# Denominators of a linear attention: summed on VectorE after a trip through DRAM, in place of a matmul

## The chip, the cores and the metric

The kernel runs on one core of one Trainium2 chip. Time is device microseconds of one execution; the verdicts compare medians of several executions of the two kernels on the same chip. Engines are named as in the profile: PE (TensorE), PEld (its weight loads), DVE (VectorE), ACT (ScalarE), POOL (GpSimd) and SP (SyncE). DVE, ACT, POOL and SP each work their instructions off in order. SP and ACT both issue DMAs; q1 is the queue of those from SP, q10 the queue of those from ACT.

## The reference

`x` is 2048 tokens of width 640. Two branches are computed from it and mixed by a gate for each token. Branch A is a linear attention with 32 heads of width 20; branch B is a token-shift MLP with two layer norms (hidden width 1728).

```
q, k, v = split(x @ wqkv);  phi(t) = where(t > 0, t+1, exp(t)) + 1e-6
kv  = sum over s of phi(k)[s,d] * v[s,e]           (a 20x20 matrix for each head)
z   = sum over s of phi(k)[s]                      (20 numbers for each head)
den = sum over d of phi(q)[s,d] * z[d] + 1e-6      (one number for each token and head)
a   = concat(phi(q) @ kv / den) @ wo
h   = gelu(layernorm(x) @ w1); four channel groups shifted by +1, -1, +2, -2 tokens
x1  = x + h_shifted @ w2;  b = x1 + gelu(layernorm(x1) @ w3) @ w4
out = g*a + (1-g)*b,  g = sigmoid(x . gate_w)
```

The change touches how `den` is summed.

## The kernel before

The tokens are 16 chunks of 128, in 4 tiles of 512 (index `t`, chunk `cc` in it). The program is written in the order in which each engine runs it; nothing is rescheduled. The stages follow each other on PE: `k_mm`, `q_unit`, `g_unit` (x against phi(k)), `w1_unit` for tiles 0 and 1 with `kv_unit` and `m_unit` (the folded matrix kv*wo in six groups) between them, `w2_unit(0, cc)`, `w1_unit` for tiles 2 and 3, and then for each tile the loop of `w3_unit`, with the next tile's `w2_unit` and this tile's `att_unit` between its pieces, and `w4_turned`.

phi(q) lies with features on partitions: partition `p` of chunk `j` (`j` is 0 to 4) holds feature 5p+j, so a head takes four neighbouring partitions. `den_add(j)` adds `z`-weighted chunks into `u`, 128 partitions x 2048 tokens of float32, which lies in the first two fifths of `xT`, out of use by then. What is left is a sum over each head's four partitions.

Before the change PE makes that sum. `den_hi` (ACT, L263) and `den_lo` (DVE, L266) split `u` into two bfloat16 parts in `xT`. `den_mm` (L272) multiplies both with the 0/1 mask `hm_bf`, built on POOL at the start, four tiles at once into four column groups of the array. `den_evac` (DVE, L278) adds 1e-6 into an `x1` buffer, with 32*t + head on partitions. `den_recip` (DVE, L283) inverts it into `r_bf`, `r_spread` copies it to `r4` on 32 partitions (DVE, L287), and four DMAs (L289) put each head's row on its four partitions in `rb`. `scale_t(0)` (DVE, L293) multiplies phi(q) of tile 0 with it, and `att_unit(0, 0)` (L518) is the first to read that.

Around these steps:

- `m_unit(g)` ends in a copy on ACT (L431). `m_store` writes the six results to DRAM (L435), `m_load` fetches them back in the layout that `att_unit` needs (L441).
- `ln1_apply` for chunks 14 and 15 runs on ACT (L329). Each normalized chunk goes through a DMA transpose issued by SP (L333) into `lnxT`, the input of `w1_unit(3)` (L396). `ln2_apply` (DVE, L504) does the same for `w3_unit` (L506, L537).
- `w4_sb` is loaded after `r_spread` (L654 to L656) and first read by `w4_turned(0)` (L568), which also needs `h2x`, transposed by a DMA at L556.
- `w4_sb` and the `x1` buffers lie over `xT` and its neighbours, so they wait for the last use of those.
- Each DMA takes the next of eight semaphores in turn, and waits until the DMA eight before it has landed.

Of the kernel before, what the change touches and what calls it, by code (L numbers as in the profile page):

```python
# [8 lines left out]
ALU = mybir.AluOpType  # L9
BF16 = mybir.dt.bfloat16  # L10
F32 = mybir.dt.float32
# [5 lines left out]
def kernel(  # L17
# [13 lines left out]
    nc = tc.nc  # L31
    P = 128
    S, D = A_x.shape[1], A_x.shape[2]
    F = B_w3.shape[1]
    H, Dh = 32, 20
    NCH = S // P
    TS = 512
    NT = S // TS
    CPT = TS // P
    DC = D // P  # L40
    HD = D // 2
    FF = F // P
    FR = F - FF * P
    EPS = 1e-5
    CG = D // 4
# [3 lines left out]
    GW = GH * Dh  # L49
    NG = 6  # L50
    row0 = [g * GW for g in range(5)] + [D - P]
# [9 lines left out]
    const = ctx.enter_context(tc.tile_pool(name="const", bufs=1))  # L61
# [4 lines left out]
    ps = ctx.enter_context(tc.tile_pool(name="ps", bufs=4, space=PSUM))  # L66
    dram = ctx.enter_context(tc.tile_pool(name="dram", bufs=1, space=bass.MemoryType.DRAM))
    m_dram = dram.tile([NG, P, D], BF16)

    def pair():  # L70
        return ps.tile([P, 2, 512], F32, name="pp")
# [7 lines left out]
    w2_sb = const.tile([P, DC, D], BF16)  # L79
    w3_sb = const.tile([P, DC, F], BF16)  # L80
    wo_sb = const.tile([P, NG, D], BF16)
# [8 lines left out]
    g5 = const.tile([DC, P], BF16)  # L90
    g5z = const.tile([P, P], BF16)
    mhalf = const.tile([P, CPT], F32)
    hmask = const.tile([P, H], F32)
    z = const.tile([P, DC], F32)
    hm_bf = const.tile([P, H], BF16)
    bmask = const.tile([P, GH * 4], F32)
    bmask5 = const.tile([P, 8], F32)
    ylog = const.tile([P, NCH], F32)
# [15 lines left out]
    xT = st1.tile([P, DC, S], BF16)  # L114
# [27 lines left out]
    load_x(2, 16)  # L142
    sp.dma_start(wv_sb[:], wqkv_v[:, :, 2 * D:3 * D])
    sp.dma_start(w1_sb[:], B_w1.rearrange("(c p) f -> p c f", p=P))
    for g in range(NG):
        sp.dma_start(wo_sb[:, g, :], A_wo[row0[g]:row0[g] + P, :])
    sp.dma_start(w2_sb[:, 0:2, :], B_w2[0:2 * CG, :].rearrange("(g p) f -> p g f", g=2)[0:P])
    for g in range(2, 4):
        sp.dma_start(w2_sb[:, g, :], B_w2[CG * g:CG * g + P, :])
    sp.dma_start(w2_sb[:, 4, :], B_w2.rearrange("(g p) f -> g p f", g=4)[:, P:CG, :])  # L150
    sp.dma_start(w3_sb[:], B_w3.rearrange("(c p) f -> p c f", p=P))

# [4 lines left out]
                            base=0, pattern=[[-1, P]], channel_multiplier=1)  # L157
    for c in range(0, NCH, CPT):
        nc.gpsimd.memset(x_sb[:, c:c + CPT, D:D + 1], 1.0)
    nc.gpsimd.memset(hmask[:], 1.0)  # L160
    nc.gpsimd.affine_select(out=hmask[:], in_=hmask[:], compare_op=ALU.is_ge, fill=0.0,
                            base=0, pattern=[[-4, H]], channel_multiplier=1)
    nc.gpsimd.affine_select(out=hmask[:], in_=hmask[:], compare_op=ALU.is_ge, fill=0.0,
                            base=3, pattern=[[4, H]], channel_multiplier=-1)
    nc.gpsimd.tensor_copy(hm_bf[:], hmask[:])
    for m, n, off in ((bmask, GH, 0), (bmask5, 2, 88)):
        nc.gpsimd.memset(m[:], 1.0)
        nc.gpsimd.affine_select(out=m[:], in_=m[:], compare_op=ALU.is_ge, fill=0.0,
# [90 lines left out]
            else:  # L259
                nc.vector.scalar_tensor_tensor(u[:, sl], pqT[:, j, sl], z[:, j:j + 1], u[:, sl], op0=ALU.mult, op1=ALU.add)  # L260

    def den_hi(sl):
        nc.scalar.copy(xT[:, 4, sl], u[:, sl])  # L263

    def den_lo(sl):
        nc.vector.tensor_tensor(xT[:, 3, sl], u[:, sl], xT[:, 4, sl], op=ALU.subtract)  # L266

    def den_mm():
        pt = pair()
        for n in range(2):  # L270
            for t in range(NT):
                nc.tensor.matmul(pt[32 * t:32 * (t + 1), 0, :], lhsT=hm_bf[:], rhs=xT[:, 4 - n, t * TS:(t + 1) * TS],  # L272
                                 start=(n == 0), stop=(n == 1))
        return pt

    def den_evac(pt):
        d = x1p.tile([P, D], F32, name="x1")[:, 0:TS]
        nc.vector.tensor_scalar_add(d, pt[:, 0, :], 1e-6)  # L278
        return d

    def den_recip(d):
        with nc.allow_low_precision(reason="rounded after a float32 division, as a copy would"):
            nc.vector.reciprocal(r_bf[:], d)  # L283
# [39 lines left out]
    def ln1_apply(c, eng=nc.vector):  # L323
        t, cc = divmod(c, CPT)
        if cc == 0:
            lnxT[t] = lnx_p.tile([P, DC, TS], BF16, name="lnxT")
        lnx = work.tile([P, D], BF16, name="ln")
        if eng is nc.scalar:
            nc.scalar.activation(lnx[:], x_sb[:, c, 0:D], ACT.Identity, bias=nmr1[:, c:c + 1], scale=rstd1[:, c:c + 1])  # L329
        else:  # L330
            nc.vector.tensor_scalar(lnx[:], x_sb[:, c, 0:D], mv1[:, c, 0:1], rstd1[:, c:c + 1],
                                    op0=ALU.subtract, op1=ALU.mult)
        nc.sync.dma_start_transpose(lnxT[t][:, :, cc * P:(cc + 1) * P], lnx[:])  # L333
# [92 lines left out]
    def m_unit(g):  # L426
        pt = pair()
        for hf in range(2):
            nc.tensor.matmul(pt[:, hf, 0:HD], lhsT=kvT[:, row0[g]:row0[g] + P],  # L429
                             rhs=wo_sb[:, g, hf * HD:(hf + 1) * HD], start=True, stop=True)  # L430
        nc.scalar.copy(mst[g // 2][:, g % 2, :].rearrange("p (h e) -> p h e", h=2), pt[:, :, 0:HD])  # L431

    def m_store():
        for i in range(NG // 2):
            nc.sync.dma_start(m_dram[2 * i:2 * i + 2].rearrange("g p e -> p g e"), mst[i])  # L435
# [7 lines left out]

    for fcs in w1_split:
        w1_unit(0, fcs)
    for sl in halves:
        den_hi(sl)
    kv_unit()
    for sl in halves:
        den_lo(sl)  # L450
    for cc in range(2, CPT):
        ln1_stat(3 * CPT + cc)
    ln1_rstd(3, 2, CPT)
# [7 lines left out]
        m_unit(g)  # L461
    w1_unit(1, w1_split[2])
    m_unit(4)
    den_ps = den_mm()
    m_unit(5)
    m_store()
    s1.close()
    w4p = ctx.enter_context(tc.tile_pool(name="w4p", bufs=1))
    w4_sb = w4p.tile([P, FF + 1, D], BF16)
    h2x_p = ctx.enter_context(tc.tile_pool(name="h2x_p", bufs=2))  # L470
    h2p = ctx.enter_context(tc.tile_pool(name="h2p", bufs=1))
    x1p = ctx.enter_context(tc.tile_pool(name="x1p", bufs=11))
    den = den_evac(den_ps)
    ln1_nmr(3, 2, CPT)
    for cc in range(2, CPT):
        ln1_apply(3 * CPT + cc, nc.scalar)
    st = {}


    def w2_unit(t, cc):  # L480
        c = t * CPT + cc
        if cc == 0:
            st[t] = dict(x1=[], mv=small.tile([P, CPT, 2], F32, name="mv2"))
        pt = pair()
        for hf in range(2):
            for fc in range(DC):
                nc.tensor.matmul(pt[:, hf, 0:HD], lhsT=hsT[:, fc, 2 + c * P:2 + (c + 1) * P],  # L487
                                 rhs=w2_sb[:, fc, hf * HD:(hf + 1) * HD], start=(fc == 0), stop=(fc == DC - 1))
        x1 = x1p.tile([P, D], F32, name="x1")
        nc.vector.tensor_tensor(x1[:].rearrange("p (h e) -> p h e", h=2), pt[:, :, 0:HD],  # L490
                                x_sb[:, c, 0:D].rearrange("p (h e) -> p h e", h=2), op=ALU.add)
        ln_stats(st[t]["mv"][:, cc, :], x1[:], small.tile([P, 2, 6], F32, name="bnst")[:])
        st[t]["x1"].append(x1)

    def ln2_rstd(t, c0, c1):
        if c0 == 0:
            st[t]["rstd"] = small.tile([P, CPT], F32, name="rstd2")
        rsqrt(st[t]["rstd"][:, c0:c1], st[t]["mv"][:, c0:c1, 1])

    def ln2_apply(t, cc):  # L500
        if cc == 0:
            st[t]["lnT"] = lnx_p.tile([P, DC, TS], BF16, name="lnxT")
        ln = work.tile([P, D], BF16, name="ln")
        nc.vector.tensor_scalar(ln[:], st[t]["x1"][cc][:], st[t]["mv"][:, cc, 0:1], st[t]["rstd"][:, cc:cc + 1],  # L504
                                op0=ALU.subtract, op1=ALU.mult)
        nc.sync.dma_start_transpose(st[t]["lnT"][:, :, cc * P:(cc + 1) * P], ln[:])  # L506

    def x1_scale(t, cc):
        c = t * CPT + cc
        x1 = st[t]["x1"][cc]  # L510
        nc.scalar.activation(x1[:], x1[:], ACT.Copy, scale=omg[:, c:c + 1])
# [129 lines left out]

    for cc in range(CPT):
        w2_unit(0, cc)
        ln2_rstd(0, cc, cc + 1)
        if cc >= 1:
            ln2_apply(0, cc - 1)
    w1_unit(2, w1_split[0])
    ln2_apply(0, CPT - 1)
    m_load()
    den_recip(den)  # L650
    r_spread()
    for fcs in w1_split[1:]:
        w1_unit(2, fcs)
    nc.sync.dma_start(w4_sb[:, 0:FF, :], B_w4[0:FF * P, :].rearrange("(c p) f -> p c f", p=P))  # L654
    nc.sync.dma_start(w4_sb[0:FR, FF, :], B_w4[FF * P:F, :])
    nc.sync.dma_start(w4_sb[FR:P, FF, :], B_w4[FF * P:F, :])  # L656
    scale_t(0)
    for fcs in w1_split:
        w1_unit(3, fcs)
    for cc in range(CPT):  # L660
        x1_scale(0, cc)
    NW3 = (FF + 1) // 2
    ahead = {0: ((1, 0),), 1: ((2, 0),), 2: ((3, 0),)}
    for t in range(NT):
        for i in range(NW3):
            if t > 0 and 2 <= i < 2 + CPT:
                w4_turned_out(t - 1, i - 2)
            w3_unit(t, i)
            for u, i0 in ahead.get(t, ()):
                if 0 <= i - i0 < CPT:  # L670
                    w2_unit(u, i - i0)
                    ln2_rstd(u, i - i0, i - i0 + 1)
                    if i > i0:
                        ln2_apply(u, i - i0 - 1)
            if 2 <= i < 2 + CPT:
                att_unit(t, i - 2)
            for u, i0 in ahead.get(t, ()):
                if i - i0 == CPT - 1:
                    ln2_apply(u, CPT - 1)
        if t < NT - 1:  # L680
            w4_turned(t)
        else:
            w4_last(t)
# [30 lines left out]
```

## Time and profile before

| | |
|---|---|
| time, median of 3 runs | 262.52 us (262.43 to 262.85) |
| the profiled execution | 262.87 us |
| its span, first to last instruction | 261.1 us |
| PE busy | 255.3 us, 98% |
| DVE, ACT, POOL busy | 147.7, 108.1, 31.9 us |
| packets of q1, share of 16 DMA engines | 44.5% |
| packets of q10 | 0.6% |

The time that lies around the span is 1.8 us. Busy time is a share of the whole span; which wait ends last at a stage is read from the chain of waits and from the timeline around that stage.

### The profile page before, as it was taken

What the parts mean: (1) busy time and instruction counts of PE and PEld (TensorE: products, weight loads), DVE (VectorE), ACT (ScalarE), POOL (GpSimd) and SP (SyncE); (2) the same over time, 40 slices, a digit from 0 to 9 for tenths busy, and PEclk for the clock granted to TensorE, in tenths of its full rate; (3) what the DMA queues carried; (4) which work ended last, traced back from release to release, by engine and by line L of the source; (5) the groups of instructions that cost most, each with busy time, mean ns of one, the idle gap of its engine ahead of it and who ended that gap; (6) DMA issues with size and microseconds to landing.
All of it is one profiled execution on the core that took longest, in us unless ns stands there. A gap on an engine that the chain in (4) does not pass through costs nothing.

```text
span 261.1 us, 4130 instructions
## 1 busy us (share of the span) xinstructions
PE 255.3 (98%) x1590; PEld 151.4 (58%) x1613; DVE 147.7 (57%) x273; ACT 108.1 (41%) x168; POOL 31.9 (12%) x87
## 2 busy tenths in 40 slices
PE   7999999999999999999999999999999999999995
PEld 3677655688855644566464565455565546465553
DVE  2488778799999789299400398600277610125132
ACT  3455444465787645522343322442322344342100
POOL 3000040023410240023000131000023000000000
PEclk9999999999999999999999999999999999999999
DMA  9999998016672776964122123314123412211011
GB/s 193 186 132 335 367 357 298 10 29 125 125 104 50 204 103 136 268 206 95 26 42 40 20 53 88 83 21 59 24 50 73 102 20 43 40 45 53 25 50 50
DMA packets 57557, 28.27 MB, mean 108 GB/s; under 512 B 45506, under 2 KB 56770, under 8 KB 57538
## 3 DMA queue, kind: packets, MB, share of 16 engines
q1 hardware_dynamic: 57096, 27.52, 44.5%
q10 hardware_dynamic: 442, 0.49, 0.6%
q8 instruction: 12, 0.20, 0.3%
q14 instruction: 7, 0.06, 0.1%
HBM read 13.03 MB, written 3.60 MB: 64 GB/s over the span
## 4 chain that ended last, share of the span: by engine, by line
PE 96%; DMA 2%; issue 1%; SPq 0%; DVE 0%
PE pp L537 21%; PE pp L576 16%; PE pp L487 8%; PE pp L341 8%; PE pp L518 8%; PE pp L241 8%; PE pp L396 8%; PE pp L190 8%; PE pp L612 5%; DMA wk_sb<-in_A_wqkv_dram 2%; PE pp L547 1%; PE pp L568 1%; PE pp L429 1%; PE pp L415 1%; SPq L123 0%
## 5 line engine op out<-in xcount | busy, mean ns | idle before, releaser
L537 PE MATMUL pp<-lnxT,w_sb 128*128 128x512 bf16 x249 | 59.8, 379 | 0.6
L539 ACT ACTIVATE h<-pp 128x1024 bf16<-128x1024 f32 (+1 forms) x28 | 26.9, 962 | 56.0 <-PE pp L537 56.0
L576 PE MATMUL pp<-h,w_sb 128*128 128x512 bf16 (+1 forms) x228 | 42.4, 343 | 0.3
L537 PEld LDWEIGHTS <-w_sb 128*128 128x128 bf16 x260 | 25.2, 98 | 26.9
L490 DVE TENSOR_TENSOR x<-pp,x_sb 128x640 f32<-128x640 f32 x16 | 13.1, 816 | 40.0 <-PE pp L487 40.0
L576 PEld LDWEIGHTS <-w_sb 128*128 128x128 bf16 x234 | 22.6, 98 | 19.5 <-issue 1.0
L182 ACT ACTIVATE e<-pp 128x640 bf16<-128x640 f32 (+1 forms) x26 | 21.4, 827 | 9.6 <-PE pp L241 9.6
L304 POOL TENSOR_SCALAR rstd<-mv 128x1 f32<-128x1 f32 (+2 forms) x22 | 9.1, 416 | 128.9 <-DVE mv L310 127.9
L518 PE MATMUL pp<-m_sb,pqT 128*128 128x320 bf16 x160 | 24.3, 299 | 0.0
L487 PE MATMUL pp<-w_sb,hsT 128*128 128x320 bf16 x160 | 23.9, 299 | 0.0
L524 DVE SCALAR_TENSOR_TENSOR x<-pp,gate,x 128x640 f32<-128x640 f32 x16 | 14.1, 882 | 17.2 <-PE pp L518 11.7
L190 PE MATMUL pp<-wk_sb,xT 128*128 128x320 bf16 (+1 forms) x160 | 22.5, 302 | 0.9 <-DMA wk_sb<-in_A_wqkv_dram 0.9
L341 PE MATMUL pp<-x_sb,pk 128*128 128x320 bf16 (+1 forms) x160 | 22.0, 300 | 0.0
L241 PE MATMUL pp<-xT,hsT 128*128 128x512 bf16 x98 | 21.6, 379 | 0.1
L341 PEld LDWEIGHTS <-pk 128*128 128x128 bf16 x160 | 18.8, 117 | 3.2
L487 PEld LDWEIGHTS <-hsT 128*128 128x128 bf16 x160 | 15.6, 98 | 8.2 <-issue 0.2
L518 PEld LDWEIGHTS <-pqT 128*128 128x128 bf16 x160 | 15.7, 98 | 7.7
L190 PEld LDWEIGHTS <-xT 128*128 128x128 bf16 x160 | 15.8, 99 | 7.3 <-issue 1.1
L589 DVE SCALAR_TENSOR_TENSOR oc<-pqT,omg,x 128x640 bf16<-128x640 bf16 x12 | 10.5, 878 | 16.8 <-DMA pqT<-hx 16.8
L396 PE MATMUL pp<-lnxT,w_sb 128*128 128x512 bf16 x77 | 17.9, 379 | 0.2
L241 PEld LDWEIGHTS <-hsT 128*128 128x128 bf16 x100 | 11.8, 118 | 9.7
L305 POOL TENSOR_TENSOR rstd<-rstd,mhalf 128x1 f32<-128x1 f32 (+2 forms) x22 | 16.8, 764 | 1.8
(90 smaller groups left out, 251.0 us busy)
## 6 DMA issues: line engine op xcount, KB each, us to landing
x_sb<-in_A_x_dram SPq DMA_DIRECT2D x1, 2240.0 KB
out_dram<-oc SPq DMA_DIRECT2D x14, 160.0 KB, 1.8
w_sb<-in_B_w_dram SPq DMA_DIRECT2D x1, 2160.0 KB
w_sb<-in_B_w_dram SPq DMA_DIRECT2D x1, 2080.0 KB
wo_sb<-in_A_wo_dram SPq DMA_DIRECT2D x6, 160.0 KB
hsT<-in_A_wqkv_dram SPq DMA_DIRECT2D x1, 800.0 KB
m_sb<-in_A_wqkv_dram SPq DMA_DIRECT2D x1, 800.0 KB, 12.4
w_sb<-in_B_w_dram SPq DMA_DIRECT2D x1, 800.0 KB
```

The costliest lines, as they stand in the source:

```text
L182: nc.scalar.activation(ev, src, ACT.Exp)
L190: nc.tensor.matmul(pt[:, hf, 0:n], lhsT=xT[:, dc, c * P:(c + 1) * P], rhs=wk_sb[:, dc, hf * HD:hf * HD + n], start=(dc == first), stop=(dc ...
L241: nc.tensor.matmul(pt[:, t % 2, :], lhsT=wq_sb[:, dc, :].rearrange("p (m j) -> p j m", j=DC)[:, j], rhs=xT[:, dc, t * TS:(t + 1) * TS], st ...
L305: nc.gpsimd.tensor_tensor(out_ap, out_ap, mhalf[:, 0:out_ap.shape[1]], op=ALU.pow)
L341: nc.tensor.matmul(pt[:, hf, 0:HD + hf], lhsT=w, rhs=x_sb[:, c, hf * HD:(hf + 1) * HD + hf], start=(c == 0), stop=(c == NCH - 1))
L396: nc.tensor.matmul(pt[:, i, :], lhsT=w, rhs=lnxT[t][:, dc, :], start=(dc == 0), stop=(dc == DC - 1))
L487: nc.tensor.matmul(pt[:, hf, 0:HD], lhsT=hsT[:, fc, 2 + c * P:2 + (c + 1) * P], rhs=w2_sb[:, fc, hf * HD:(hf + 1) * HD], start=(fc == 0), ...
L518: nc.tensor.matmul(pt[:, hf, 0:HD], lhsT=pqT[:, j, c * P:(c + 1) * P], rhs=m_sb[:, j, hf * HD:(hf + 1) * HD], start=(j == 0), stop=(j == D ...
L524: nc.vector.scalar_tensor_tensor(x1, pt[:, :, 0:HD], gate[:, c:c + 1], x1, op0=ALU.mult, op1=ALU.add)
L537: nc.tensor.matmul(pt[:, k, :], lhsT=w3_sb[:, dc, fc * P:(fc + 1) * P], rhs=lnT[:, dc, :], start=(dc == 0), stop=(dc == DC - 1))
L539: nc.scalar.activation(h2[:, 2 * i * TS:(2 * i + n) * TS], pt[:].rearrange("p h e -> p (h e)")[:, 0:n * TS], ACT.Gelu_apprx_tanh)
L576: nc.tensor.matmul(dst, lhsT=w4_sb[:, fc, d * P:(d + 1) * P], rhs=st[t]["h2"][:, fc * TS + a:fc * TS + b], start=False, stop=(fc == FF - 1))
```

## The change

- `u` is no longer split and multiplied. `den_store` writes it to DRAM (1 MB, float32), by a DMA that ACT issues after the last `w1_unit(0)` piece. `den_load` reads it back by four DMAs, issued by ACT: the i-th brings feature 4h+i of each head h to partition 32*t + h, so that the four features of a head stand side by side in four `x1` buffers. `den_sum` adds them on DVE in three instructions, with the 1e-6. `den_recip` and what follows are as before.
- The mask, its POOL instructions, `den_hi`, `den_lo`, `den_mm` and `den_evac` are gone.
- `m_unit(5)`, `m_store`, `den_load` and `ln1_apply` for chunks 14 and 15 now stand after `w2_unit(0, 0)`.
- The loads of `w4_sb` move behind `w2_unit(1, 1)`, in the first tile's loop.
- The six loads of `wo_sb` become three, those of `w2_sb` chunks 0 to 3 one in place of three.

```diff
+    u_dram = dram.tile([P, S], F32)
...
-    for g in range(NG):
-        sp.dma_start(wo_sb[:, g, :], A_wo[row0[g]:row0[g] + P, :])
-    sp.dma_start(w2_sb[:, 0:2, :], B_w2[0:2 * CG, :].rearrange("(g p) f -> p g f", g=2)[0:P])
-    for g in range(2, 4):
-        sp.dma_start(w2_sb[:, g, :], B_w2[CG * g:CG * g + P, :])
+    sp.dma_start(wo_sb[0:GW, 0:5, :], A_wo[0:5 * GW, :].rearrange("(g p) e -> p g e", p=GW))
+    sp.dma_start(wo_sb[GW:P, 0:5, :], ...)
+    sp.dma_start(wo_sb[:, 5, :], A_wo[row0[5]:row0[5] + P, :])
+    sp.dma_start(w2_sb[:, 0:4, :], B_w2.rearrange("(g p) f -> p g f", g=4)[0:P])
     sp.dma_start(w2_sb[:, 4, :], B_w2.rearrange("(g p) f -> g p f", g=4)[:, P:CG, :])
...
-    def den_hi(sl):   ...   def den_lo(sl):   ...   def den_mm():   ...   def den_evac(pt):   ...
+    def den_store():
+        nc.scalar.dma_start(u_dram[:], u)
+
+    def den_load():
+        parts = []
+        for i in range(4):
+            d = x1p.tile([P, D], F32, name="x1")[:, 0:TS]
+            nc.scalar.dma_start(d, u_dram[:].rearrange("(h i) (t e) -> i t h e", i=4, t=NT)[i])
+            parts.append(d)
+        return parts
+
+    def den_sum(parts):
+        a, b, c, d = parts
+        nc.vector.tensor_tensor(a, a, b, op=ALU.add)
+        nc.vector.scalar_tensor_tensor(c, c, 1e-6, d, op0=ALU.add, op1=ALU.add)
+        nc.vector.tensor_tensor(a, a, c, op=ALU.add)
+        return a
...
-    for sl in halves:
-        den_hi(sl)
+    den_store()
     kv_unit()
-    for sl in halves:
-        den_lo(sl)
...
     m_unit(4)
-    den_ps = den_mm()
-    m_unit(5)
-    m_store()
     s1.close()
...
-    den = den_evac(den_ps)
     ln1_nmr(3, 2, CPT)
-    for cc in range(2, CPT):
-        ln1_apply(3 * CPT + cc, nc.scalar)
...
         w2_unit(0, cc)
+        if cc == 0:
+            m_unit(5)
+            m_store()
+            u4 = den_load()
+            for c in range(2, CPT):
+                ln1_apply(3 * CPT + c, nc.scalar)
...
-    den_recip(den)
+    den_recip(den_sum(u4))
...
-    (the three loads of w4_sb)
+    def load_w4(): (the same three)
...
+                    if u == 1 and i == i0 + 1:
+                        load_w4()
```

More of the change, by code (lines that the diff above doesn't have):

```diff
@@ L92 @@
     mhalf = const.tile([P, CPT], F32)
-    hmask = const.tile([P, H], F32)
     z = const.tile([P, DC], F32)
-    hm_bf = const.tile([P, H], BF16)
     bmask = const.tile([P, GH * 4], F32)
@@ L144 @@
     sp.dma_start(w1_sb[:], B_w1.rearrange("(c p) f -> p c f", p=P))
-    for g in range(NG):
-        sp.dma_start(wo_sb[:, g, :], A_wo[row0[g]:row0[g] + P, :])
-    sp.dma_start(w2_sb[:, 0:2, :], B_w2[0:2 * CG, :].rearrange("(g p) f -> p g f", g=2)[0:P])
-    for g in range(2, 4):
-        sp.dma_start(w2_sb[:, g, :], B_w2[CG * g:CG * g + P, :])
+    sp.dma_start(wo_sb[0:GW, 0:5, :], A_wo[0:5 * GW, :].rearrange("(g p) e -> p g e", p=GW))
+    sp.dma_start(wo_sb[GW:P, 0:5, :], A_wo[D - 5 * GW:D, :].rearrange("(g p) e -> p g e", p=GW)[2 * GW - (D - 5 * GW) - GW:P - (D - 5 * GW)])
+    sp.dma_start(wo_sb[:, 5, :], A_wo[row0[5]:row0[5] + P, :])
+    sp.dma_start(w2_sb[:, 0:4, :], B_w2.rearrange("(g p) f -> p g f", g=4)[0:P])
     sp.dma_start(w2_sb[:, 4, :], B_w2.rearrange("(g p) f -> g p f", g=4)[:, P:CG, :])
@@ L159 @@
         nc.gpsimd.memset(x_sb[:, c:c + CPT, D:D + 1], 1.0)
[L160 to L165, printed above, removed]
     for m, n, off in ((bmask, GH, 0), (bmask5, 2, 88)):
@@ L260, in den_add @@
                 nc.vector.scalar_tensor_tensor(u[:, sl], pqT[:, j, sl], z[:, j:j + 1], u[:, sl], op0=ALU.mult, op1=ALU.add)
[L262 to L279, printed above, removed]
+    def den_store():
[13 more added lines that the diff above has]
+        return a
     def den_recip(d):
@@ L653 @@
         w1_unit(2, fcs)
-    nc.sync.dma_start(w4_sb[:, 0:FF, :], B_w4[0:FF * P, :].rearrange("(c p) f -> p c f", p=P))
-    nc.sync.dma_start(w4_sb[0:FR, FF, :], B_w4[FF * P:F, :])
-    nc.sync.dma_start(w4_sb[FR:P, FF, :], B_w4[FF * P:F, :])
     scale_t(0)
@@ L661, with load_w4 @@
         x1_scale(0, cc)
+    def load_w4():
+        nc.sync.dma_start(w4_sb[:, 0:FF, :], B_w4[0:FF * P, :].rearrange("(c p) f -> p c f", p=P))
+        nc.sync.dma_start(w4_sb[0:FR, FF, :], B_w4[FF * P:F, :])
+        nc.sync.dma_start(w4_sb[FR:P, FF, :], B_w4[FF * P:F, :])
     NW3 = (FF + 1) // 2
```

## The prediction

> **What bounds the kernel now.** I read the page first, then the chain, PE's waits, and the timeline and one-microsecond windows around the change.
>
> ```profile
> span 261.1 us, 4130 instructions
> PE 255.3 (98%) x1590; PEld 151.4 (58%) x1613; DVE 147.7 (57%) x273; ACT 108.1 (41%) x168; POOL 31.9 (12%) x87
> ...
> PE 96%; DMA 2%; issue 1%; SPq 0%; DVE 0%
> ```
>
> The chain is PE from 6.9 us to the end, so an edit earns only the PE time it removes, and costs the time by which it makes PE wait. PE's waits list one wait after the start, 0.9 us at L190. Everything else lands in time, some of it narrowly. The timelines of 66 to 90 and 90 to 150 us show how narrowly (start, length, engine, line):
>
> ```profile
> 77.61 1.98 ACT L263 CAST xT<-xT 128x1024 bf16<-128x1024 f32 x2
> ...
> 79.84 2.35 DVE L266 TENSOR_TENSOR xT<-xT 128x1024 bf16<-128x1024 f32 x2
> ...
> 85.20 0.61 PE L272 MATMUL pp<-xT,hm_bf 128*32 128x512 bf16 x8
> ...
> 88.41 1.73 ACT L329 ACTIVATE ln<-x_sb,nmr,rstd 128x640 bf16<-128x640 bf16 x2 [1.04 <-issue]
> ```
>
> ```profile
> 97.06 4.48 PE L396 MATMUL pp<-lnxT,w_sb 128*128 128x512 bf16 x20
> ...
> 98.19 0.61 DVE L504 TENSOR_SCALAR ln<-x,mv,rstd 128x640 bf16<-128x640 f32 x1 [0.76 <-POOL rstd L305]
> 98.72 3.34 DVE L283 RECIPROCAL r_bf<-x 128x512 bf16<-128x512 f32 x1
> ...
> 102.10 1.17 DVE L287 COPY r<-r_bf 32x512 bf16<-32x512 bf16 x4
> ...
> 109.51 1.49 DVE L293 TENSOR_TENSOR pqT<-pqT,rb 128x2560 bf16<-128x2560 bf16 x1 [5.02 <-DMA rb<-r]
> ...
> 113.01 1.52 PE L518 MATMUL pp<-m_sb,pqT 128*128 128x320 bf16 x10
> ```
>
> Three deadlines follow. `w1_unit(3)` starts at 97.06 and needs the transposes of chunks 14 and 15, of which the last landed at 95.74: 1.3 us to spare. `att_unit(0, 0)` starts at 113.01, scale_t(0) ends at 111.0: 2.0 us. `w4_turned(0)` starts at 128.03, its last input (h2x) landed at 122.6: 5.4 us.
>
> The windows from 36 us on show a load like the new ones: w2's fifth chunk (L150, issued at 35.35), whose DRAM side is split 4 x 32 rows as in den_load.
>
> ```profile
> 36.00:37.00 1.00, 1.00 (x7) 0.51 (x6) 0.90 (x2) 0.00 (x0) 1.00 (x7) 1.00 1.03 355
> ...
> 42.00:43.00 1.00, 1.00 (x6) 0.54 (x5) 0.90 (x3) 0.31 (x1) 0.00 (x0) 1.00 1.03 404
> 43.00:44.00 1.00, 1.00 (x6) 0.57 (x5) 1.00 (x1) 0.55 (x1) 0.00 (x0) 1.00 1.01 394
> 44.00:45.00 1.00, 1.00 (x7) 0.51 (x6) 0.53 (x2) 0.47 (x1) 0.00 (x0) 1.00 0.47 183
> 45.00:46.00 1.00, 1.00 (x6) 0.56 (x5) 0.97 (x1) 0.40 (x1) 0.16 (x2) 1.00 0.29 114
> ```
>
> The last two columns are the busy share of the 16 DMA engines and GB/s. The w3 load queued behind L150 should end everywhere at once; instead the share falls to 0.29, 4.6 engines, for over a microsecond: a few engines had more to do. The semaphores say the same. A load over 128 partitions lands in sixteen steps. L150 had four (40.54, 40.81, 41.74, 42.13) after one at its issue. m_load's pieces of 24 partitions had twelve, and of the rb load behind them four shares landed at 105.7 to 106.3 and twelve from 107.4: it is always the same engines that are used.
>
> **What goes.** den_mm takes 0.55 us of the chain (L272, 85.27 to 85.82): -0.55 us. ACT loses 1.98 us (L263), DVE 2.35 (L266) and 0.69 (L278), POOL four small instructions at the start; PE waits for none of these. DVE's freed 2.35 us brings chunks 12 and 13 and m_store's first two pieces some 2 us forward. The merged wo and w2 loads carry the same bytes, POOL's and PE's readers come far later, and SP saves five issues of 0.43 us while the DMA engines are full: 0.
>
> **den_store.** 1 MB, issued at 77.7, when ACT has finished L403. All 16 engines; at the 344 GB/s that m_store reached (window 90 to 91), 3 us after a start of 1.3. It lands near 83, with the engines idle from 81 to 85; its first reader comes at 88. Cost 0; if it took 10 us, den_load would start that much later.
>
> **den_load.** ACT reaches it after m_unit(5)'s copy, which moves behind w2_unit(0, 0): PE 85.27 + 1.36 + 0.4, ACT to 87.95. Four issues of 0.44 (L129) to 0.72 us (L150), I take 0.6, hold ACT to 90.35. Behind them wait the two ln1_apply, 0.87 each: done at 91.2 and 92.1 in place of 89.3 and 90.1. SP issues their transposes at 91.3 and 92.5; 1.3 us later they move. The next work on ACT, w1_unit(2)'s gelu at 94.0, has room.
>
> The loads carry 512 rows of 2 KB. If like L150 they run on four engines, that is 128 rows each. In window 45 to 46 an engine moved 114/4.6 = 24.7 GB/s: 83 ns for a row, 10.7 us in all from 89.3, to 100.0. L150's own packets went at 78 ns for 1,280 bytes: 125 ns for a row, 16 us. I take 83, since only the stragglers worked there, and keep 125 for the range.
>
> [...]
>
> On those four engines q1's packets wait their turn. Between 3.5 and 5.5 us, with both queues full, q1 moved 261 and q10 264 packets of 1,280 bytes: one for one. A transpose is 640 packets of 256 bytes, 40 an engine, 20 ns each. Turn by turn with rows it takes 40 x 0.103 = 4.1 us in place of 0.8, and transposes run in order:
>
> - chunk 14: 92.6 to 96.7; chunk 15: to 100.8, landed 101.1.
> - w1_unit(3) now wants it at 97.06 - 0.55 = 96.5. PE waits **4.6 us**.
> - den_load: 28 rows by 92.6, 80 more by 100.8, the last 20 by 102.9, landed 103.2. By the turn of the semaphores SP's first two m_load issues wait for the third and fourth of these landings; six issues of 0.43 us end at 105.8, before rb's are due: 0.
>
> **The denominators' path.** DVE reaches den_sum at 98 and waits for 103.2. Queued behind it are the reciprocal, the hx copies of tile 2 and scale_t. Three additions of 0.63 us (half of L266's 1.22 us), 3.34 and 1.17: r4 at 109.6. Before, r4 to the last rb landing took 6.1 us, with m_load in the way; one such load lands in 4.8. So scale_t ends at 116.0 to 117.3. att_unit(0, 0), 4.6 late, comes at 117.06: 0 to 0.3 us, but its 2 us of cover are gone.
>
> **w4's load.** SP issues it behind the transpose of chunk 4, 8.4 us after rb lands, 1.3 us to start, 2.29 MB at 365 GB/s (windows 108 to 114) 6.4 us, and h2x behind it in q1, 1.8 us with the transpose in between: 17.9 us after rb, 132.3 to 133.6. w4_turned(0) wants it at 128.03 + 4.05 = 132.1. Cost 0.2 to 1.5 us.
>
> **The clock.** A 4.6 us gap can cost PE its clock. In this trace the record falls to 0.5 at 261.6, 3.2 us after the last matmul, and the first five 512-column matmuls take 2.29 us where warm ones take 0.215 each. If that speed lasts 4 us, the cost is **2 us**, and the late rb and h2x are hidden in it. [...]
>
> **The sum.** 4.6 + 2.0 - 0.55 = 6.0 us on the profiled 262.87, 0.35 above the median; on 262.52, 268.5 us. About 0.5 us (0.2%) is what a measurement here can tell from no change.
>
> **Rivals.** *The loads spread over all engines* (the other side): 1 MB at 350 GB/s is 3 us. All landed by 94, the transposes by 96.5, den_sum starts at 98 as DVE gets there. rb lands where it did, and -0.55 is left: 262.0 us. It decides if den_load lands before 98 and chunk 15 before 96.5. Against it are L150's landings.
> *Short packets pass the long ones*: transposes are hardly held and chunk 15 lands by 96. Then den_load goes last: q1's 5 us are served within its 10.7, landed 105.3, scale_t 118.1 to 119.4. att_unit waits 5.7 to 6.9, h2x 0.8, the clock 2 us: 270.5 to 272.
> *Dear rows*, 125 ns: a transpose takes 5.8 us, chunk 15 lands at 104.5, 8 us of waiting and 2 of clock: 272.
> *The cover is larger than I think* and den_load only nibbles at it: with chunk 15 by 97.5 and rb as before, 1 us of w1_unit and 0.5 of h2x against 0.55: 262.5 to 264.
>
> **How the numbers follow.** The forecast 0.55, passing packets 0.18, dear rows 0.15, nibbling 0.06, spread loads 0.06. Without the clock's 2 us the forecast is 266.5; with a cheap landing 265. The range of 264.0 to 273.0 leaves out spread loads, most of nibbling and the top of the dear ones. Faster 0.06, same 0.03 (half of nibbling), slower 0.91.
>
> **What would show it.** In the profile after: q10 with some 1,100 packets and its share near 3%; windows from 93 to 103 us with DMA shares of 0.3 to 0.6 and under 200 GB/s; PE waiting at L387, the new w1_unit, for lnxT, 3 to 8 us; DVE waiting 3 us or more for x at den_sum; an rb landing near 115; PE's clock below 1.0 after the gap. I am wrong if den_sum finds its data, if PE waits nowhere in 96 to 130, or if the wait is at w4 alone.

## The result

The changed kernel takes 271.96 us (median of 6 runs, 270.54 to 272.58) against 262.48 us for the kernel before on the same chip: 1.0358 times, with a 95% interval of 1.0328 to 1.0388. That is 9.5 us slower. The forecast was 268.5, with a range of 264 to 273: side and range held, the forecast was 3.5 us too low.

The profiled execution took 271.61 us. Its page (span, busy time, queues, chain):

```profile
span 269.5 us, 4111 instructions
PE 256.9 (95%) x1582; PEld 151.9 (56%) x1605; DVE 146.8 (54%) x273; ACT 106.4 (39%) x166; POOL 30.9 (11%) x83
...
PEclk9999999999999975999999999999999999999999
...
q10 hardware_dynamic: 1114, 2.59, 2.7%
...
PE 94%; DMA 4%; issue 1%; DVE 0%
```

The chain is still PE's, but 4% of it is now a DMA (2% before), and PE's clock has a dent that it did not have. PE's waits name the place, and the chain the DMA (start, length):

```profile
PE pp L387 <- DMA lnxT<-ln: 7.7, 1, 7.7
```

```profile
90.17 1.89 PE pp L387 x8
92.05 10.85 DMA lnxT<-ln
102.90 0.14 issue
103.03 1.01 PE pp L387 x2
```

L387 is `w1_unit` and the wait is in front of `w1_unit(3)`, for the transpose of chunk 15. The timeline around it (start, length, engine, line) has the whole loss:

```profile
86.02 3.68 ACTq L261 DMA_DIRECT2D x<-u_dram  x4
...
89.80 1.73 ACT L320 ACTIVATE ln<-x_sb,nmr,rstd 128x640 bf16<-128x640 bf16 x2 [3.25 <-DVE x L472]
...
90.75 3.06 SPq L324 DMA_TRANSPOSE lnxT<-ln  x2
...
103.03 6.88 PE L387 MATMUL pp<-lnxT,w_sb 128*128 128x512 bf16 x20 [7.74 <-DMA lnxT<-ln]
103.56 0.69 DVE L267 TENSOR_TENSOR x<-x,x 128x512 f32<-128x512 f32 x1
...
114.86 1.49 DVE L284 TENSOR_TENSOR pqT<-pqT,rb 128x2560 bf16<-128x2560 bf16 x1 [3.48 <-DMA rb<-r]
...
121.38 1.52 PE L500 MATMUL pp<-m_sb,pqT 128*128 128x320 bf16 x10
```

PE waits 7.74 us, and the 20 matmuls behind the wait take 6.88 us where 20 like them took 4.48 before: 2.40 more. With den_mm's 0.55 taken off that is 9.6 us, and 9.5 were measured. (This execution's span is only 8.4 us longer mainly because PE's wait for wk at the start, 0.91 us in the execution before, happened not to occur. Its early times lie about 1 us ahead of the forecast's.) The windows show the four engines and then the clock (the last three columns are PE's clock, the busy share of the DMA engines, and GB/s; packets count in the window in which they start, so held ones can push the share over 1):

```profile
91.00:92.00 1.00, 1.00 (x6) 0.48 (x5) 0.96 (x3) 0.53 (x1) 0.48 (x1) 1.00 0.28 103
92.00:93.00 1.00, 1.00 (x7) 0.41 (x5) 0.97 (x3) 0.90 (x2) 0.28 (x1) 1.00 4.03 200
93.00:94.00 1.00, 1.00 (x6) 0.46 (x5) 0.97 (x3) 0.18 (x1) 0.76 (x2) 1.00 0.27 104
...
98.00:99.00 1.00, 0.00 (x0) 0.00 (x0) 0.00 (x0) 0.00 (x0) 0.00 (x0) 0.50 1.24 123
```

Window 92 to 93 is the strange one. The trace's packets say what happened there. Some 400 of chunk 14's 640 packets of 256 bytes went in the 0.7 us from 91.9 on, most in some 20 ns each. Then 16 packets that started between 92.45 and 92.63 all ended between 95.79 and 95.91: the transpose stood nearly still for 3.35 us while den_load's rows went on, 143 of them in this time, most in 84 ns. From 96 to 99 both moved, some 170 short packets and 41 rows in each microsecond.

### The profile page after: what moved, and what is told of

Read it like the earlier page. It is cut to its first block, busy times and chain, and to the rows that moved or that the text cites. A ratio compares the mean times of both kernels' runs of the same rounds, so it can differ in the third digit from the quotient of the medians.

```text
span 269.5 us, 4111 instructions
## 1 busy us (share of the span) xinstructions
PE 256.9 (95%) x1582; PEld 151.9 (56%) x1605; DVE 146.8 (54%) x273; ACT 106.4 (39%) x166; POOL 30.9 (11%) x83
## 4 chain that ended last, share of the span: by engine, by line
PE 94%; DMA 4%; issue 1%; DVE 0%
PE pp L519 21%; PE pp L558 16%; PE pp L182 8%; PE pp L332 8%; PE pp L469 8%; PE pp L500 8%; PE pp L233 8%; PE pp L387 8%; PE pp L594 5%; DMA lnxT<-ln 4%; PE pp L195 1%; PE pp L529 1%; PE pp L550 1%; PE pp L420 1%; PE pp L406 1%
## 5 line engine op out<-in xcount | busy, mean ns | idle before, releaser
L519 PE MATMUL pp<-lnxT,w_sb 128*128 128x512 bf16 x249 | 59.8, 379 | 0.6
L519 PEld LDWEIGHTS <-w_sb 128*128 128x128 bf16 x260 | 25.2, 98 | 26.8
L558 PEld LDWEIGHTS <-w_sb 128*128 128x128 bf16 x234 | 22.7, 98 | 19.5 <-issue 1.0
L387 PE MATMUL pp<-lnxT,w_sb 128*128 128x512 bf16 x77 | 20.3, 416 | 7.9 <-DMA lnxT<-ln 7.7
L387 PEld LDWEIGHTS <-w_sb 128*128 128x128 bf16 x80 | 8.2, 104 | 18.5 <-DMA x<-u_dram 8.2
```

What stands on the lines that cost most here:

```text
L387: nc.tensor.matmul(pt[:, i, :], lhsT=w, rhs=lnxT[t][:, dc, :], start=(dc == 0), stop=(dc == DC - 1))
L519: nc.tensor.matmul(pt[:, k, :], lhsT=w3_sb[:, dc, fc * P:(fc + 1) * P], rhs=lnT[:, dc, :], start=(dc == 0), stop=(dc == DC - 1))
L558: nc.tensor.matmul(dst, lhsT=w4_sb[:, fc, d * P:(d + 1) * P], rhs=st[t]["h2"][:, fc * TS + a:fc * TS + b], start=False, stop=(fc == FF - 1))
```

## Experiments

The theory to be tried: den_load's four busy engines hold up the transposes of chunks 14 and 15, these hold up PE, and the wait halves PE's clock. Rivals: the order of issue on ACT, the trip's volume, the denominators' new path on VectorE, w4's late load. Each kernel ran beside the kernel before on its chip (262.38 us for the first four, 261.85 for the next four, 261.80 for the last two), so ratios are compared.

**The loads spread over 16 engines (e1_spread).** The same bytes, issues and places.

```diff
-    u_dram = dram.tile([P, S], F32)
+    u_dram = dram.tile([4, P, TS], F32)
-        nc.scalar.dma_start(u_dram[:], u)
+        for i in range(4):
+            nc.scalar.dma_start(u_dram[i].rearrange("(t h) e -> h t e", t=NT),
+                                u[bass.ds(i, H, 4), :].rearrange("h (t e) -> h t e", t=NT))
-            nc.scalar.dma_start(d, u_dram[:].rearrange("(h i) (t e) -> i t h e", i=4, t=NT)[i])
+            nc.scalar.dma_start(d, u_dram[i])
```

> The changed kernel, with the sum stored in four pieces so that each of the four loads reads 128 rows that lie one after the other and can be split 16 ways; the bytes, the four load issues, their place and the work on VectorE stay. If four busy engines are the cause (theory): den_load lands within 5 us of its issue, the transposes of chunks 14 and 15 land by 96.5, PE waits under 1 us at w1_unit(3), the clock stays at 1.0, and -0.55 us for den_mm is left: 261.5 to 263 us. If the two late issues of those transposes behind four DMA issues on ACT are the cause (rival order): a wait of 3 us or more stays and the time is 266 or more. If the 2 MB of extra traffic is the cause (rival volume): 266 or more as well, with long waits while the 16 engines are all busy.

Measured: 262.91 us, 1.0027 (1.0008 to 1.0045). Windows, and PE's waits:

```profile
90.00:91.00 1.00, 1.00 (x9) 0.71 (x8) 0.97 (x3) 0.99 (x2) 0.50 (x1) 1.00 1.07 394
91.00:92.00 1.00, 0.95 (x6) 0.44 (x5) 0.96 (x4) 0.00 (x0) 0.48 (x1) 1.00 1.06 406
```

```profile
PE pp L182 <- DMA wk_sb<-in_A_wqkv_dram: 1.4, 1, 1.4
PE pp L552 <- DMA h2x<-hx: 0.8, 1, 0.8
```

Each load now lands in sixteen steps, the last by 93.03. Chunks 14 and 15 land by 94.51 and 95.09, the clock stays at 1.0 and the wait at `w1_unit(3)` is gone, with the four issues still ahead of the two ln1_apply. So neither the order on ACT nor the volume makes the 9.5 us. A wait at w4's first matmuls (L552) shows in place of it; see below.

**ln1_apply ahead of den_load (e2_turn_first).**

```diff
-            u4 = den_load()
             for c in range(2, CPT):
                 ln1_apply(3 * CPT + c, nc.scalar)
+            u4 = den_load()
```

> The changed kernel with the two ln1_apply of chunks 14 and 15 (and so their transposes) ahead of den_load on ACT; den_load stays on its four engines. Theory: the transposes meet only the first rows, chunk 15 lands by 96 and PE waits 0 to 1.5 us at w1_unit(3); the four transposes of ln2 and the denominators take the delay over: den_load lands near 103 to 105, rb near 115 to 117, att_unit(0, 0) waits 2 to 4 us: 264 to 267 us. Rival order: with the order undone all is undone, 262 us. Rival volume: no better than the changed kernel, 270 or more.

Measured: 271.91 us, 1.0364 (1.0333 to 1.0395): no gain. It misses the theory's 264 to 267 as well as the order rival's 262; the volume rival's 270 or more fits, but e1_spread has ruled that one out. ACT's queue issued the first load at 86.97, while ACT was still in the first ln1_apply (86.71 to 87.63), and SP issued the transposes when the ln1_apply had ended, at 87.66 and 89.66. So the edit moved the transposes forward by 3 us, but not past the loads, and the rival order is not ruled out by this run; e1_spread does that. Their packets were held from 89.7 to 93.4, and chunk 15 landed at 102.93 as before. Issuing 3 us earlier did not help: the transposes met the running loads all the same and were held for 3.7 us.

**PE kept busy in the wait (e3_keep_clock).**

```diff
     scale_t(0)
+    wpt = pair()
+    warmup(34, TS, wpt)
     for fcs in w1_split:
         w1_unit(3, fcs)
```

> The changed kernel with 34 matmuls of 512 columns on a constant ahead of w1_unit(3), 34 x 0.215 = 7.3 us of PE work that fills the wait for lnxT. If the halved clock after the wait costs 2.4 us (20 matmuls of w1_unit(3) took 6.88 in place of 4.48 us): the clock stays at 1.0, L387 takes 4.5 us again, and the time is 269.0 to 270.0. If the clock costs nothing that the wait does not hide: 271.5 to 272.5. If the wait is shorter in unprofiled runs than 7.3 us: slower than 272.

Measured: 270.27 us, 1.0307 (1.0282 to 1.0331), 1.7 us below the changed kernel's median.

```profile
96.10 7.60 PE L195 MATMUL pp<-const-bfloat16-1.0 128*128 128x512 bf16 x33
105.34 4.48 PE L387 MATMUL pp<-lnxT,w_sb 128*128 128x512 bf16 x20 [1.65 <-DMA lnxT<-ln]
```

The matmuls of `w1_unit(3)` are back at 4.48 us and the clock is 1.0 throughout, so the 2.4 us are the clock's. The gain between the medians is smaller, and the time lies 0.3 us above the range expected. In the profiled execution, the longest of the five (271.14 us), the transposes were held a second time, from 100.8 to 102.0, and chunk 15 landed only at 105.21; a 16 KB load of the instruction queue, which took 3.46 us, ended within that hold. Whether the other four executions met the same is not known.

**The loads twice (e4_twice).** The second set goes into w4's empty buffer and is not read.

```diff
                 ln1_apply(3 * CPT + c, nc.scalar)
+            for i in range(4):
+                nc.scalar.dma_start(w4_sb[:].rearrange("p c d -> p (c d)")[:, 2 * TS * i:2 * TS * (i + 1)].bitcast(F32),
+                                    u_dram[:].rearrange("(h i) (t e) -> i t h e", i=4, t=NT)[i])
```

> The changed kernel with the four loads issued a second time, into w4's still empty buffer, behind the two ln1_apply on ACT; the copies are not read. It doubles the rows on the four engines to 256 each. If the engines take turns between the two queues (theory): the transposes of chunks 14 and 15 land where they did, 102.9, the wait at w1_unit(3) stays 7 to 9 us, and only what comes later (ln2's transposes, m_load, rb, each at 4 us and more) moves: 272 to 277 us. If the ACT queue's rows go ahead of SP's packets (rival): the transposes wait for all 256 rows, 21.5 us from 87.5, w1_unit(3) waits some 17 us and the time is 281 or more.

Measured: 281.71 us, 1.0739 (1.0701 to 1.0776).

```profile
PE pp L387 <- DMA lnxT<-ln: 9.6, 1, 9.6
PE pp L519 <- DMA m_sb<-m_dram: 4.1, 1, 4.1
```

The total is in the rival's range, but for another reason than the rival's. The wait at `w1_unit(3)` grew by 1.9 us, not by ten, so the rows did not go ahead of the transposes. Nor did the transposes land where they had, as the theory said, but one after the other at the slow pace: chunks 14 and 15 and ln2's first two transposes landed at 102.30, 106.05, 109.90 and 113.74: 3.75, 3.85 and 3.84 us apart, which is the forecast's 4.1 us for a transpose against waiting rows. The rest is mostly a second wait, at w3's first unit, with a second fall of the clock behind it (0.5 from 117.95 to 121.37). The view names m_sb, but the transpose of ln2's chunk 3 had landed only at 118.04, and PE went on at 118.28. I had given what comes after `w1_unit(3)` more room than it has.

**w4's load back in its place, loads spread (e5_spread_w4).**

```diff
+    (the three loads of w4_sb, after w1_unit(2))
     scale_t(0)
...
-                    if u == 1 and i == i0 + 1:
-                        load_w4()
```

> The kernel of e1_spread (loads over 16 engines) with w4's load back at its place ahead of scale_t(0). In e1_spread PE waited 0.8 us for h2x at w4's first matmuls and nowhere else after the start. Theory: that wait is the price of the later w4 load and goes, the 0.55 us of den_mm stay gone: 261.7 to 262.3 us, 0.6 to 0.9 under e1_spread and 0.1 to 0.7 under before. Rival: the stored and reloaded sum costs PE something by itself: no better than e1_spread, 262.9.

Measured: 261.77 us, 1.0005 (0.9976 to 1.0035). L552's wait is gone from the profile and nothing replaces it:

```profile
PE pp L182 <- DMA wk_sb<-in_A_wqkv_dram: 0.8, 1, 0.8
PE pp L195 <- PEq L694: 0.8, 1, 0.8
```

`w1_unit(3)` starts at 96.56 here and at 97.06 before, although k's matmuls resumed 0.32 us later (7.21 against 6.89): den_mm's half microsecond is gained on PE. In the time it can't be told from no change. Two of the twelve executions took 264.7 us at a granted clock of 0.99, so PE may still lose some clock now and then; no trace shows where.

**Half of the loads (e6_half).**

```diff
-        for i in range(4):
+        for i in range(2):
             d = x1p.tile([P, D], F32, name="x1")[:, 0:TS]
...
-        return parts
+        return [parts[0], parts[1], parts[1], parts[1]]
```

> The changed kernel with only two of the four loads (features 0 and 1); the additions use the second one three times, so the denominators are other numbers, with the same work on VectorE. 64 rows for each of the four engines in place of 128, all read 5.4 us after 87.5, or 94 with m_store's packets in between. Theory (the transposes wait only as long as rows are there): chunk 15 lands by 96.5, PE waits 0 to 1 us, the clock stays at 1.0: 262.3 to 264 us. Rival (the hold of 3.4 us that the first transpose met comes once whatever the amount): chunk 14 lands at 96.5, chunk 15 at 97.5 to 98, PE waits 2 to 3 us: 264.5 to 266.

Measured: 266.09 us, 1.0141 (1.0107 to 1.0176), just above the rival's time, with a wait of 3.13 us against its 2 to 3. The theory's 0 to 1 us is missed.

```profile
98.59 6.16 PE L387 MATMUL pp<-lnxT,w_sb 128*128 128x512 bf16 x20 [3.13 <-DMA lnxT<-ln]
```

Half the rows, and the first transpose was again held for 3.4 us (90.1 to 93.5). Chunk 14 landed at 97.94, chunk 15, with the rows gone, 0.5 us later. The hold did not shrink with the amount: 3.4 us against 3.35. This wait of 3.13 us also cost clock, 6.16 against 4.48; in one of the four executions (264.18 us) the granted clock stayed at 1.0.

**The loads behind the transposes, in their queue (e7_sp_behind).** As e2_turn_first, and issued by SP:

```diff
-            nc.scalar.dma_start(d, u_dram[:].rearrange("(h i) (t e) -> i t h e", i=4, t=NT)[i])
+            nc.sync.dma_start(d, u_dram[:].rearrange("(h i) (t e) -> i t h e", i=4, t=NT)[i])
```

> The changed kernel with the four loads issued by SP behind the transposes of chunks 14 and 15: the same four engines and bytes, but in the transposes' own queue and after them. Theory: with no second queue to take turns with, chunk 15 lands by 94 and PE does not wait at w1_unit(3). ln2's four transposes stand behind the loads and land by 107; den_load lands at 103 to 104.5, rb at 115 to 117, so att_unit(0, 0), due at 113.0 - 0.55, waits 3 to 5 us, h2x 0.8: 264.5 to 268 us. Rival (four busy engines hold any work that needs all 16, in whatever order): 270 or more.

Measured: 269.47 us, 1.0291 (1.0258 to 1.0324). Chunks 14 and 15 land by 90.01 and 91.32 and `w1_unit(3)` does not wait, as expected. The wait has moved to ln2's transposes behind the loads; the chain:

```profile
92.00 11.76 DMA x<-u_dram
103.75 3.12 DMA lnxT<-ln
106.87 0.09 issue
106.96 3.24 PE pp L519 x8
```

```profile
96.00:97.00 1.00, 1.00 (x7) 0.43 (x5) 0.61 (x1) 0.00 (x0) 0.14 (x1) 1.00 7.49 200
```

The time is above my range because I had w3's first unit due near 113, with att_unit; it is due at 100.6, when `w1_unit(3)` ends. The 7.49 in the window is the clearest sight of the hold: 15 transpose packets started between 96.49 and 96.64 and ended at 103.76 to 103.80, just as the last load landed (103.87 to 103.91). In between rows alone moved, 24 in half a microsecond at 84 ns each, four at a time. The packet records name no engine: that twelve free engines ran ahead with the first ln2 transpose and then stood still until the four had come to it is my reading of these numbers, and was not shown.

**The trip alone, on the kernel before (e8_dead_trip).** den_mm and the order stay; nothing reads the loads.

```diff
+    nc.scalar.dma_start(u_dram[:], u)
     for sl in halves:
         den_hi(sl)
...
+    h2d = h2p.tile([P, FF * TS], BF16, name="h2")
+    for i in range(4):
+        nc.scalar.dma_start(h2d[:, 2 * TS * i:2 * TS * (i + 1)].bitcast(F32),
+                            u_dram[:].rearrange("(h i) (t e) -> i t h e", i=4, t=NT)[i])
     for cc in range(2, CPT):
         ln1_apply(3 * CPT + cc, nc.scalar)
```

> The kernel before, with den_mm and all its work in place, and the trip added as dead traffic: u is stored at the same point, and the four loads on four engines go into h2's still empty buffer, ahead of the two ln1_apply on ACT. Nothing reads them. Theory (the trip's traffic is the whole cost): PE waits 7 to 9 us at w1_unit(3), the clock halves, 271 to 274 us. Rival (the cost lies in the denominators' new path on VectorE, in the moved m_unit(5) or in w4's late load): 262.5 to 265.

Measured: 272.55 us, 1.0409 (1.0384 to 1.0434), with the changed kernel's wait:

```profile
PE pp L397 <- DMA lnxT<-ln: 7.7, 1, 7.7
```

The traffic alone, with none of the other edits, costs what the whole change costs and, by the ratios, some 1.3 us more, of which den_mm's 0.55 us, not saved here, is a part; the rest is not accounted for. The denominators' path, the moved m_unit(5) and w4's late load are not needed for it.

**w4's late load alone, on the kernel before (e9_w4_late).** The three loads moved as in the change.

> The kernel before with one part of the change alone: the three w4 loads issued where the change issues them, behind ln2's transpose of chunk 4. rb lands there at 107.5 to 109, as in e1_spread. Theory: h2x's transpose is issued behind the w4 load's 6.4 us of traffic and PE waits 0.5 to 1.2 us at w4's first matmuls, as in e1_spread (0.85): 262.4 to 263.2 us with a median of before near 262. Rival: the move is free, within 0.2 us of before, and e1_spread's wait came from something else.

Measured: 262.54 us, 1.0018 (1.0002 to 1.0035). The time is in the theory's range, but the profile does not show the theory's wait at w4's first matmuls: they start at 128.22, with h2x just in time (landed at 128.08). With e1_spread (0.85 us of wait) and e5_spread_w4 (none), the later load costs 0 to 0.85 us. It sits at the edge of what is covered.

**Rows half as long (e10_short_rows).**

```diff
-            nc.scalar.dma_start(d, u_dram[:].rearrange("(h i) (t e) -> i t h e", i=4, t=NT)[i])
+            nc.scalar.dma_start(d[:, 0:TS // 2], u_dram[:].rearrange("(h i) (t e) -> i t h e", i=4, t=NT)[i][:, :, 0:TS // 2])
+            nc.gpsimd.memset(d[:, TS // 2:TS], 1.0)
```

> The changed kernel with the first half of each row loaded only: 512 rows of 1 KB in place of 2 KB on the same four engines, so half the bytes as in e6_half, but as many rows as in the changed kernel; the other half of the denominators is set to ones by POOL and so is wrong. What is tried is what the first transpose's hold and the slow pace go by. If engines take turns packet by packet and the hold is some 40 rows that were already queued: a row costs about 45 ns, the hold shrinks from 3.4 to about 1.8 us, a transpose then takes 40 x 0.065 = 2.6 us; chunk 15 lands near 97 and PE waits 1 to 2 us: 263.5 to 265.5. If both go by time or bytes: hold 3.4 us and 4 us for a transpose as in e6_half, a wait of 3 us: 265.5 to 267.

Measured: 266.36 us, 1.0166 (1.0139 to 1.0192), a wait of 2.80 us. Time and wait are those of the second expectation. A row of 1 KB took 46 ns, but the hold was 3.2 us (92.0 to 95.2), in which 260 rows passed, 65 on an engine, where 143 of 2 KB, 36 on an engine, had passed in the changed kernel. So it is not a fixed number of rows either.

What makes the first hold stays open. It was 3.2 to 3.9 us with the loads in ACT's queue, for all, half and twice the rows and for short ones, 5.2 us in e8_dead_trip, and 0.6 to 1.8 us in the kernels without them (before, e1_spread, e5_spread_w4, e9_w4_late). One thing was the same in all eight kernels with loads on four engines: 401 to 403 packets of the transpose had started when the hold set in. What sets that number was not tried.

## Why the prediction was right, and where it was off

- **den_load on four engines, 84 ns a row**: right, by what L150's landings had shown. Each load landed in four steps after one at issue; rows took 84 ns (forecast 83); the last landed at 102.70 (forecast 103.2). e1_spread shows that this is what costs.
- **Turns between the queues, 4.1 us for a transpose**: right in the steady state (3.75 to 3.85 us in e4_twice; about 170 short packets in a microsecond, 42 on the four engines if all sixteen had the same share, against 41 rows). The counts that the prediction drew on are off: from 3.5 to 5.5 us 245 packets of 1,280 bytes of q1 and 275 of q10 started, not 261 and 264, which is still near one for one. They bear out near equal turns there, not how many rows make one turn. By equal turns alone the first transpose would have moved on at once; the hold of 3.35 us shows that they are not all of it.
- **The wait of 4.6 us**: the term that was too small; 7.7 were measured. Two things were left out for chunk 14. m_store's third piece stood ahead of it in SP's queue, and its share on the four engines landed at 92.89 only. And the transpose was held for 3.35 us, with sixteen packets open. The hold is what counts: in e2_turn_first the third piece had landed whole by 89.07, the hold was there, and chunk 15 landed no earlier. Chunk 14 took from 91.9 to 100.85 in place of 4.1 us. Chunk 15 then found the rows nearly gone and landed 2.05 us later. So chunk 15 landed at 102.90 where 101.1 was forecast, and PE, about 1 us ahead of the forecast's times, stood at 95.3. I had priced a transpose as work that each engine does for itself; then most of chunk 14's sixteen landings would have come early, as only the four engines had rows. All sixteen came between 99.68 and 100.85. After a first burst of 403 packets and the hold, some 170 of its packets went in a microsecond beside 41 rows.
- **ACT's four issues**: 3.68 us against 2.4, the fourth taking 1.87 by itself. The start of the execution hid it, and e2_turn_first shows that it did not matter.
- **The clock, 2 us**: right in kind and nearly in size, 2.4 in the row and 1.7 in e3_keep_clock. Half speed lasted 4.9 us of work; the forecast's 4 stood in no trace.
- **The denominators' path, 0 to 0.3 us**: its times held (den_sum at 103.56, scale_t ended at 116.35; the additions took 0.68 to 0.69 us each, not 0.63), and it cost 0. One sign named for it did not show: DVE did not wait for den_load's data but, just ahead of den_sum, in `ln2_apply` for the late transposes (5.96 and 1.43 us). att_unit(0, 0) came at 121.38, 5.0 us behind, because PE was later than forecast.
- **w4's late load, 0.2 to 1.5 us**: 0 here. h2x landed at 134.22, and w4_turned(0) began at 136.4. Without the other delay it is up to 0.85.
- **den_mm, -0.55, and den_store, 0**: both right. The store landed by 80.7, with 5 us to spare.
- **Rivals**: spread loads gave 262.91 where they were made (262.0 forecast, plus the w4 wait). Dear rows named 272 with 8 us of waiting, which is what was measured, but rows were not dear (84 ns). Passing packets named 270.5 to 272, which the time fits too, but it had chunk 15 land by 96, and it landed at 102.90. So the time alone speaks for these two rather than for the forecast's own 268.5; the landing of chunk 15 and the rows' 84 ns decide against them. Nibbling fell with 7.7 us.

## What to carry to other kernels

Read a transfer's price from the number of engines that it runs on, not from its bytes. With 4 x 32 rows on its DRAM side, 1 MB landed in four steps a load and took 12 us even where it ran nearly alone (e7_sp_behind, first row at 91.4, last landing at 103.9); with 128 x 1 the same bytes, issued from 87.2 on, landed in sixteen steps a load, all by 93.03 (e1_spread). The load in four steps slowed the DMA transposes beside and behind it: with rows in the other queue they landed 3.75 to 3.85 us apart (e4_twice), and packets of one behind the loads stayed open for 7.3 us (e7_sp_behind), where the 640 packets of one with no load beside it took 0.93 us (56.27 to 57.20 in the kernel before). Ask what stands behind such a load in every queue, DMA transposes above all, and let the store write the layout that the load wants, when it can be hidden. Where one engine is busy for 98% of the span, an edit can earn only what it takes off that engine, here half a microsecond; in the profiled executions a wait at `w1_unit(3)` cost the wait and another 1.7 to 2.4 us of clock where it was 2.80 to 9.6 us long (e10_short_rows, e6_half, e8_dead_trip, the changed kernel, e4_twice), and no clock where it was 1.65 us (e3_keep_clock).

## What was not expected of the hardware

- Beside den_load, chunk 14's transpose took from 91.9 to 100.85, and all its sixteen landings were late (99.68 and after), though each of the four loads landed in four steps only. In e7_sp_behind, behind the loads, packets of a transpose stayed open for 7.3 us, until the loads were done.
- The burst was 401 to 403 packets in all eight kernels with such a load. Behind it the transpose was held 3.2 to 3.9 us (5.2 in e8_dead_trip) where the load was in the other queue, whatever the load's length or row size; the reason was not found.
- The clock fell to half 2.4 us after PE's last matmul (95.3 to 97.68) and was full again 4.9 us after work resumed (103.03 to 107.92). In e6_half the wait of 3.1 us was over when the clock fell, 1.2 us into the new work (98.59 to 99.79). Behind a wait it stayed at half for 10.24 us here and in e2_turn_first, 6.83 us in e7_sp_behind and e8_dead_trip, and 3.41 us in e6_half and e10_short_rows: three times, twice and once 3.41 us. What a wait cost did not go by its length alone: 2.80 us cost 1.7 us of clock in e10_short_rows, 7.7 us cost 2.4 here and 2.0 in e8_dead_trip. What makes the clock fall and come back at these times was not shown.
